# A written instruction list moved by a few places, and tiles handed out in turn, in a fused S5 and linear-attention kernel

## The chip, the core and the metric

The kernel runs on one core of one Trainium2 chip. The metric is device microseconds (us) of one execution. A core has TensorE (PE, matmuls, with its weight loads shown as PEld), VectorE (DVE), ScalarE (ACT), GpSimd (POOL) and SyncE (SP, which here only issues DMAs); POOL and ACT issue DMAs as well. Each engine works through its own instructions in their order and waits on semaphores for the others.

## The reference

One input x (2048 x 512, bf16) goes through two branches, and a gate per row mixes them:

```python
def _A_ref(x, Lambda_re, ..., Dskip):            # S5: a complex diagonal recurrence over 2048 steps
    dt = jnp.exp(log_dt)
    Lam_bar = jnp.exp(dt * Lam)
    B_bar = ((Lam_bar - 1.0) / Lam)[:, None] * Bmat
    Bu = jnp.einsum("bld,pd->blp", x + 0j, B_bar)
    for t in range(L):
        h = Lam_bar[None, :] * h + Bu[:, t, :]
    y = 2.0 * jnp.einsum("blp,dp->bld", hseq, Cmat).real + x * Dskip[None, None, :]

def _B_ref(x, wqkv, w_phi, wo):                  # linear attention, 32 heads of 16
    q, k, v = ...                                # x @ wqkv
    phi_q = concat([softmax(q @ w_phi), softmax(-q @ w_phi)])
    phi_k = concat([softmax(k @ w_phi), softmax(-k @ w_phi)])
    kv = einsum("bhsf,bhsd->bhfd", phi_k, v);  z = phi_k.sum over s
    o = (phi_q kv) / (phi_q z + 1e-6)
    return o @ wo

g = sigmoid((x * gate_w).sum(-1))
out = g * _A_ref(...) + (1 - g) * _B_ref(...)
```

## The kernel before

Everything stays on the chip between the loads at the start and the writes of the output at the end. Sequence rows are handled in 16 tiles of 128. Branch B's k, v and q come from matmuls of such tiles (`tile_mm`, L493); the feature maps work on groups of up to four tiles (`x`, `n`, `e`, `s` steps: trees of maxima and minima L544, differences L555 and L561, one exponential of 128x2048 on ACT L567, sums L575 to L586, logarithm and reciprocal L590 and L594). Branch A's input matmuls are the `b` and `g` steps (L637, L649 and on); its recurrence runs over every eighth row with scans (`z`), and the rows between are filled in by products with powers of the transition (`h`, `H`, `p`). At the end, per tile, `y` makes branch A's output in PSUM (L871, and the Dskip term with the diagonal matrix Dd, L878), `o` the attention's numerator and denominator (L890 to L903), `O` transposes that result by a DMA on SP's queue (oT<-on, L926), `t` multiplies it by Wo on top of y's bank (L939) and scales it into the output tile (L943 to L947), and `R` writes a pair of tiles out (L955, 256 KB, on SP's queue). The feature maps of q are transposed by a DMA on the same queue too (phT<-EE, L613), in the `S` steps.

What sets the order: each step is a Python generator (`st_y`, `st_t` and so on), and `ORDER` (lines 24 to 52) is a written list of 849 words. For each word the program runs the step of that name on to its next `yield`:

```python
for tok in ORDER.split():
    tok, _, banks = tok.partition("@")
    tok, _, eng = tok.partition(":")
    sel["eng"] = "dve" if eng == "D" else "act"
    sel["banks"] = [int(b) for b in banks]
    next(st[tok])
```

So `c3:D` runs the next part of `c3` with its copy on DVE, `c3` with it on ACT, and `y8@0` opens `y8` on PSUM bank 0. All engines' schedules are manual: each engine executes its instructions in the order in which the list issues them, its DMAs included. Two helpers choose the engine: `evac` (a PSUM copy, L136 on ACT, L138 on DVE) and `scaled` (a product by a per-partition scalar, L444 on ACT, L446 on DVE). `add_by_dma` (L529) adds into a tile by a DMA on POOL's queue.

At the start, small steps prepare branch A's parameters: `V` and `V2` transpose small vectors on TensorE and copy them (L330/L332, L337/L339), `P` and others compute with them on ACT and DVE, `M2` makes the products of powers on POOL (L421 to L429, nine operations, of which L425 writes scalars that the `c` steps read), and `Dk` makes Dd from Drow on POOL (L343); Drow is the row Dskip, loaded by DMA.

Tiles of five pools ("feat", "tabtmp", "ssm", "featQ", "outp") are asked from their pool each time, which rotates over a fixed number of buffers per name and waits until the buffer's last user is done.

Of the kernel before, what the change touches and what calls it, by code (L numbers as in the profile page):

```python
# [24 lines left out]
B:D Lk Lk Z@0 Lx Z Z Z Z Z Z W00@1 Z B B B W01@2 W01 W01:D W00 W00 W10@0 Lx W11@3 Lx T0@4 B W11 T0 f1@2 Lx Lx f0@1 f0  # L25
W10:D f1:D T1@5 T1:D f2@3 f2 V2@1 V2 f3@0 f3:D k0@6 x0z:D Lx k1@7 V@3 V P U U k1 k1 k0 k0 P k3@3 P2 P P2 U P2 U k6@2 P2
P2 x0 Lx Lb Lx Lb P4 n0 P4 k3 x0 P4 P3 i3 P2 n0 P3 k5@7 x0 i3 x0 Lc k5 k9@3 k9 i0 Ld Dk k2@0 M n0 i3 i3 k10@1 i3 k4@3 i0
M k2 i0 i0 i0 M Lb k10 i2 M k6 n0 k4 k7@0 k7 i2 Lb k8@7 i1 i2 x0 i1 i1 k13@6 M2 k11@0 n0 i2 k8 i1 x1 n1 x1 D n1 x1
b200@1 i2 i1 L i0:D x1 D c1:D n1 Lc Lc i3:D n1 k11 e0 b010@7 b010 c0:D x1 n1 i2:D b200 x2 s0 c0:D s0 k12@3 k12 x2 g200@2
g200 n2 c1 b100@0 s0 b100 x2 b001@5 n2 Lv b000@7 Lc i1 b000 b111@4 b111 x2 n2 s0 n2 g000@2 b001 s0 c3:D b011@3 b101@7 e1  # L30
x2 n2 g000 g000 Lx g001@5 g001 x3 s1 v1@4 b011 c3 s0 c2:D c2:D c1:D k14@2 g010@3 g010 Lo e2 x3 n3 s1 k13 D v0@0 v1 s1
g011@1 x3 c3:D g011 x3 g001 g011 v0 e2 k15@0 g011 g010 c0:D Lq Lq g010 s1 n3 k14 w2@6 c3 s0 D k15 n3 a0@54 s2 a0 g011 x3
n3 g011 Ld g010 g201@2 b101 Ld n3 s1 w2 g010 z0 b201@1 b201 z0 b110@7 n4 s1 x4 g101@3 g201 l2:D s2 s2 x4 n4 e3 z0 z0
w1@6 w1 b110 g100@2 g100 g101 g101 g100 s2 s2 s2 g111@1 l2:D l2:D g111 n4 g110@0 g110 e3 g110 g111 v2@2 v3@3 x4 n4 g110
g111 g111 g110 l2:D z0 v2 z0 v3 w3@2 s1 z0 g111 s3 g110 w0@7 w3 a1 a1 x4 c1 g301@6 z0 z1 z1 x4 w0 c2 g301 s3 g300@2 g300
z0 q3@7 q3 n4 e4 v5@6 z0 s2 s2 q2@2 s3 e4 q0@7 q0 z1 z1 l2:D z1 H0:D z1 s3 z1 z1 s4 v4@3 v4 q2 q1@0 H0 z1 v7@1 q1 X0 s3
q7@7 q7 z1 s4 N0 X0 v6@3 b300@0 N0 H0 b301@7 H0:D H0 N0 X0 v6 N0 s3 a2 v5 a2 c0 a2 v7 a2 X0 b301 s3 b300 q4@1 l3:D l3:D
l3 c2 X0 N0 H1 H1:D H1:D q4 s4 q5@0 l3 q5 q6@7 g210@6 q6 X1 N1 h0:D H1:D E0 b211@0 X1 s4 E0 b210@7 X1 s3 b210 b311@1
b310@3 g211@2 s4 N1 S0 b211 N1 S0 s4 s4 l3:D X1 g311@7 N1 s4 g210 g210 b310 g211 g211 H1 g310@3 h0 h0 h0 g210 h1:D g211
g210 h1 b311 g211 g210 h0 g211 z2 z2 S0 z2 z2 z2 z2 g311 h1 g311 g311 h1 g310 g310 g310 S0 p00 v9@2 z2 g310 g310 g311  # L40
g311 v8@6 v15@1 S0 z2 z3 v10@7 p00 v12@3 v9 v8 S0 S0 v15 v11@6 z3 z2 z2 H2 v10 q11@2 p00:D z3 z3 z3 H2 a3 a3 H2 v12 z3
H2 H2 v11 h2 p10:D z3 z3 S0 z3 a3 a3 z3 p01 X1 h1 H3 q8@3 H3 H3 q10@6 q10 v14@7 h2 h2 H3 H3 v13@1 v13 p00:D S0 h2 q11 a4
v14 N1 q9@6 h2 q9 h3:D h3:D q12@1 a4 q8 h3 q12 X2 p10 E1 E1 a4 a4 Y S0 h3 h3 Y X2 G q13@3 q13 G Y Y y1@1 y0@0 y0 N2 END
p01 y0 o0@6 p00 p11 o0 S1 o1@4 o1 q15@2 o0 p10 p10 X2 y3@3 S0 y1 p11 S1 o0 X2 N2 q15 o1 S1 o2@6 o2 N2 o2 S1 S1 y3 N2 o1
# [33 lines left out]
def kernel(  # L78
# [128 lines left out]
    ft = ft_g.__enter__()  # L207
# [69 lines left out]
    tabp = tab_g.__enter__()  # L277
    iot = tabp.tile([P, NC], F32, name="iot", bufs=1)
# [258 lines left out]
    def tree(src5, L, op, nm, key, groups=NB):  # L537
        t = ft.tile([P, 4, groups, Dh // 2, 4], BF16, name=nm)[:, 0:L]
        cur = src5
        n = Dh // 2  # L540
        while n:
            last = n == 1 and op == ALU.add
            dst = ft.tile([P, 4, groups, 1, 4], F32, name="smf", bufs=2)[:, 0:L] if last else t[:, :, :, 0:n, :]
            VT(out=dst, in0=cur[:, :, :, 0:n, :], in1=cur[:, :, :, n:2 * n, :], op=op)  # L544
# [25 lines left out]
    def feat_sum(p, L, ph=None):  # L570
        EE = live["EE", p]
        E5 = EE.rearrange("p l hh s (f hl) -> p l (hh s) f hl", f=Dh)
        sq = ft.tile([P, 2, 4 * 2 * NB, 16], BF16, name="sq")[:, :, 0:L * 2 * NB]
# [11 lines left out]
        dst = ft.tile([P, 4, 2 * NB, 1, 4], F32, name="smf", bufs=2)[:, 0:L]  # L585
# [3 lines left out]
        lg = ft.tile([P, 4, 2 * NB, 1, 4], F32, name="lg", bufs=2)[:, 0:L]  # L589
        aexp(out=lg, in_=live["sm", p], func=ACT.Ln)  # L590
        yield
        if ph is None:
            rc = ft.tile([P, 4, 2 * NB, 1, 4], BF16, name="rc", bufs=2)[:, 0:L]
            aexp(out=rc, in_=lg, func=ACT.Exp, scale=-1.0)  # L594
# [104 lines left out]
    def st_z(j):  # L699
# [17 lines left out]
        w = sw.tile([P, 2, NC], BF16, name="w")  # L717
# [17 lines left out]
    def st_h4(j):  # L735
# [3 lines left out]
        mc = sw.tile([P, 2, NC], BF16, name="mc")  # L739
# [5 lines left out]
        ms = sw.tile([P, 2, NC], BF16, name="ms")  # L745
# [22 lines left out]
    def st_h(j):  # L768
# [15 lines left out]
        m5 = sw.tile([P, 2, 2, NC], BF16, name="m5")  # L784
        n5 = sw.tile([P, 2, 2, NC], BF16, name="n5", bufs=1)
# [96 lines left out]
    def st_o(n):  # L882
# [18 lines left out]
        if u == 0:  # L901
            live["on", g_] = op_.tile([P, 2, 2, 16, Dh], BF16, name="on")
# [27 lines left out]
    def st_t(n):  # L930
# [4 lines left out]
        if u == 0:  # L935
            live["ot", g_] = pools["op"][1].tile([P, 2, D], BF16, name="ot")
        for py, (c, w) in zip(pys, [(0, D)] if len(pys) == 1 else LASTCUT):
            for g in range(HG):
                MM(out=py[:], lhsT=oT[:, g, :], rhs=Wo[:, g, c:c + w], start=False, stop=(g == HG - 1))  # L939
# [79 lines left out]
```

## Time and profile before

| | |
|---|---|
| median of 3 runs | 151.36 us (151.04 to 152.04) |
| profiled execution | 151.59 us, its span 149.9 us |
| granted TensorE clock | 1.0 |
| PE busy | 140.1 us, 94% of the span |
| DVE busy | 135.3 us, 90% |
| ACT busy | 123.5 us, 82% |
| POOL busy | 45.7 us, 30% |
| chain of waits, by engine | PE 34%, DVE 30%, ACT 12%, SP's queue 10%, DMA 7% |

The profile shows one execution. Its span goes from the first to the last instruction; 1.69 us of the execution's time lie around it. Busy shares are means over stages with different limits, so they are read by windows of time. The chain of waits is followed back from the last instruction, at each step to what released it. A wait row such as "A <- B: total, times, longest" names the instruction that waited and what came last for it.

### The profile page before, as it was taken

How to read it: one execution, taken by the hardware profiler on the slowest of the kernel's cores; microseconds unless marked ns; L12 is line 12 of the kernel's file. 1: busy time of each engine (PE TensorE's matmuls, PEld its weight loads, DVE VectorE, ACT ScalarE, POOL GpSimd, SP SyncE). 2: the span in 40 equal slices, each digit the busy share in tenths (PEclk: the TensorE clock that was granted, in tenths of full speed). 3: DMA queues.
4: the chain of work that ended last, by engine and by line, in shares of the span. 5: the costliest groups of instructions: out<-in, count | busy, mean ns of one | idle time of the engine just before them, and what ended most of it. 6: DMA issues, size and time to landing. Idle time of an engine off the chain costs nothing.

```text
span 149.9 us, 2750 instructions
## 1 busy us (share of the span) xinstructions
PE 140.1 (94%) x950; PEld 71.8 (48%) x950; DVE 135.3 (90%) x330; ACT 123.5 (82%) x222; POOL 45.7 (30%) x60
## 2 busy tenths in 40 slices
PE   6799999999799999999999998999999599999990
PEld 2644444433444644554444654545455254545650
DVE  2789979999999999999999999999999997868841
ACT  3469999899999999999999999999999958922110
POOL 7300074000229095978448163051011003000000
PEclk9999999999999999999999999999999999999999
DMA  4999999970674868679977969959998999989543
GB/s 117 221 197 195 170 201 226 215 188 0 163 120 49 127 91 119 69 112 164 154 105 132 149 83 192 155 94 164 210 219 133 104 262 158 201 162 258 112 127 118
DMA packets 56014, 22.61 MB, mean 151 GB/s; under 512 B 44736, under 2 KB 54848, under 8 KB 56000
## 3 DMA queue, kind: packets, MB, share of 16 engines
q1 hardware_dynamic: 47584, 15.05, 51.9%
q0 software_dynamic: 7472, 7.08, 33.0%
q10 hardware_dynamic: 944, 0.31, 0.8%
q8 instruction: 7, 0.11, 0.3%
q14 instruction: 7, 0.06, 0.1%
HBM read 2.51 MB, written 2.10 MB: 31 GB/s over the span
## 4 chain that ended last, share of the span: by engine, by line
PE 34%; DVE 30%; ACT 12%; SPq 10%; DMA 7%; issue 3%; POOL 2%; DVEq 0%
PE PS L871 16%; PE PS L939 9%; SPq L235 6%; DMA oT<-on 4%; DVE mn L544 4%; DVE EE L555 3%; DVE mx L544 3%; DVE EE L597 3%; DVE EE L561 3%; DVE sq L575 3%; PE PS L890 3%; DMA Drow<-in_A_Dskip_dram 3%; ACT EE L567 2%; ACT vx L136 2%; SPq L241 2%
## 5 line engine op out<-in xcount | busy, mean ns | idle before, releaser
L567 ACT ACTIVATE EE<-EE 128x2048 bf16<-128x2048 bf16 x16 | 30.1, 1918 | 0.5 <-DVE EE L561 0.4
L493 PE MATMUL PS<-WKV,xT 128*128 128x488 bf16 (+1 forms) x128 | 29.4, 374 | 0.3 <-ACT H L136 0.2
L493 PEld LDWEIGHTS <-xT 128*128 128x128 bf16 x192 | 18.4, 98 | 20.9 <-issue 1.8
L136 ACT CAST Xq<-PS 128x488 bf16<-128x488 f32 (+1 forms) x32 | 17.5, 592 | 0.2
L939 PE MATMUL PS<-Wo,oT 128*128 128x512 bf16 (+2 forms) x68 | 15.5, 367 | 1.6 <-DMA oT<-on 1.6
L649 PE MATMUL PS<-xT,BT 128*128 128x512 bf16 x64 | 16.3, 379 | 0.2 <-ACT Bn L136 0.2
L871 PE MATMUL PS<-C,H 128*128 128x512 bf16 x64 | 15.6, 379 | 0.0
L493 PE MATMUL PS<-Wq,xT 128*128 128x480 bf16 x64 | 14.9, 365 | 0.6 <-ACT vx L136 0.5
L637 PE MATMUL PS<-xT,BT 128*128 128x512 bf16 x64 | 14.8, 379 | 0.0
L903 DVE TENSOR_TENSOR on<-PS,rd 128x512 bf16<-128x512 f32 x16 | 10.9, 690 | 2.0 <-ACT rd L897 1.9
L529 POOL DMA_DIRECT2D eb<-dg x4 | 4.8, 1201 | 22.7 <-ACT dg L444 11.2
L945 ACT ACTIVATE ot<-PS,G 128x512 bf16<-128x512 f32 (+1 forms) x10 | 6.3, 648 | 6.2 <-PE PS L939 6.2
L529 POOL DMA_DIRECT2D C<-CT x4 | 6.9, 1728 | 12.8 <-DVE CT L446 12.8
L939 PEld LDWEIGHTS <-oT 128*128 128x128 bf16 x68 | 6.3, 98 | 8.5 <-DMA oT<-on 2.2
L561 DVE TENSOR_TENSOR EE<-mn,Xq 128x2048 bf16<-128x2048 bf16 (+1 forms) x9 | 9.9, 1105 | 0.0
L575 DVE TENSOR_TENSOR sq<-EE 128x2048 bf16<-128x2048 bf16 (+1 forms) x9 | 10.0, 1107 | 0.0
L555 DVE TENSOR_TENSOR EE<-Xq,mx 128x2048 bf16<-128x2048 bf16 (+1 forms) x9 | 9.9, 1105 | 0.0
L637 PEld LDWEIGHTS <-BT 128*128 128x128 bf16 x64 | 6.3, 98 | 7.7 <-issue 0.3
L597 DVE TENSOR_TENSOR EE<-EE,rc 128x2048 bf16<-128x2048 bf16 x8 | 9.7, 1221 | 0.0
L649 PEld LDWEIGHTS <-BT 128*128 128x128 bf16 x64 | 6.1, 98 | 7.2 <-issue 0.5
L894 ACT ACTIVATE ld<-PS 128x32 f32<-128x32 f32 x16 | 3.0, 201 | 8.0 <-PE PS L890 6.3
L136 ACT CAST vx<-PS 128x512 bf16<-128x512 f32 x16 | 9.3, 606 | 0.0
(193 smaller groups left out, 322.5 us busy)
## 6 DMA issues: line engine op xcount, KB each, us to landing
out_dram<-ot SPq DMA_DIRECT2D x7, 256.0 KB, 2.6
C<-CT POOLq DMA_DIRECT2D x4, 256.0 KB, 5.2
eb<-CT POOLq DMA_DIRECT2D x4, 256.0 KB, 4.5
eb<-dg POOLq DMA_DIRECT2D x4, 256.0 KB, 4.1
sq<-sq POOLq DMA_DIRECT2D x3, 256.0 KB, 4.0
WKV<-in_B_wqkv_dram SPq DMA_DIRECT2D x1, 512.0 KB, 4.8
Wo<-in_B_wo_dram SPq DMA_DIRECT2D x1, 512.0 KB, 3.9
WKV<-in_A_x_dram SPq DMA_DIRECT2D x2, 256.0 KB, 4.1
```

The costliest lines, as they stand in the source:

```text
L136: nc.scalar.copy(out=out_ap, in_=in_ap)
L493: MM(out=pt[:], lhsT=xT[:, kt, ti * P:(ti + 1) * P], rhs=W[:, kt, :], start=(kt == 0), stop=(kt == KT - 1))
L529: nc.gpsimd.dma_start(out=out_ap, in_=in_ap, accum_op=ALU.add)
L555: VT(out=half(EE, 0), in0=X5, in1=live["mx", p].to_broadcast([P, L, 8, Dh, 4]), op=ALU.subtract)
L561: VT(out=half(live["EE", p], 1), in0=live["mn", p].to_broadcast([P, L, 8, Dh, 4]), in1=X5, op=ALU.subtract)
L567: aexp(out=EE[:, l_:l_ + 2], in_=EE[:, l_:l_ + 2], func=ACT.Exp)
L575: VT(out=sq.rearrange("p q x i -> p x q i"), in0=e4[:, :, 0:2], in1=e4[:, :, 2:4], op=ALU.add)
L597: VT(out=E5[:, u:u + 2], in0=E5[:, u:u + 2], in1=rc[:, u:u + 2].to_broadcast([P, 2, 2 * NB, Dh, 4]), op=ALU.mult)
L637: MM(out=pb[:], lhsT=BT[:, ri, kt, j * P:(j + 1) * P], rhs=cells(kt, 2 * pr), start=(kt == 0), stop=(kt == KT - 1))
L649: MM(out=pgq[:], lhsT=BT[:, ri, kt, js], rhs=cells(kt, r1), start=(kt == 0), stop=(dst == 0 and j in LJ and kt == KT - 1))
L871: MM(out=py[:], lhsT=hs[j][ri], rhs=C2[:, 1 - ri, j, c:c + w], start=(j == 0 and ri == 0), stop=False)
L939: MM(out=py[:], lhsT=oT[:, g, :], rhs=Wo[:, g, c:c + w], start=False, stop=(g == HG - 1))
```

## The change

Two things change.

First, the five pools' tiles. A new helper, `rotating`, takes each name's buffers from the pool once and hands them out in turn; the number of buffers per name is the same. The later transposed feature maps get a name of their own (`phq`), and the output tile `ot` is asked for after the matmuls of `st_t`.

Second, `ORDER`. It holds the same 849 words. 264 stand at the same place, 304 one place away, 262 two, 15 three to five; four move by more (the copy of `k9` by 18 places back, `Dk` by 38 back and so behind `M2`, the copy of `k2` by 6 and `R2` by 6 forward), and the first `c3` changes its copy engine from DVE to ACT. Three steps get another PSUM bank (`V2`, `k4`, `v0`).

```diff
-W10:D f1:D T1@5 T1:D f2@3 f2 V2@1 V2 f3@0 f3:D k0@6 x0z:D Lx k1@7 V@3 V P U U k1 k1 k0 k0 P ...
+W10:D T1@5 f2@3 f1:D V2@6 V2 T1:D f2 f3@0 f3:D x0z:D k0@6 V@3 V Lx k1@7 U U P k1 k1 k0 k3@3 k0 ...
...
-o6 R0 o7@2 p20 y4 y4 o7 N3 p01 o6 o6 p20 o7 o7 y5@5 p30 E3 y5 O2 E3 y5 p20 S2 y8@0 t5 t4 p30:D y11@1 S2 R1 o9@2 p20 p20
+S2 o6 o7@2 R0 y4 o7 p20 p01 y4 N3 o6 o6 p20 o7 o7 E3 p30 y5@5 y5 y5 E3 O2 y8@0 p20 S2 y11@1 t4 t5 p30:D R1 S2 p20 p20
...
+    def rotating(pool, bufs0):
+        slots = {}
+
+        def tile_of(shape, dtype, name, bufs=None):
+            s = slots.setdefault(name, [[], 0])
+            if not s[0]:
+                s[0] = [pool.tile(shape, dtype, name=f"{name}{k}", bufs=1) for k in range(bufs or bufs0)]
+            s[1] += 1
+            return s[0][(s[1] - 1) % len(s[0])]
+
+        return tile_of
...
-    ft = ft_g.__enter__()
+    ft_tile = rotating(ft_g.__enter__(), 1)
...
-    def enter(key, **kw):
-        g = tc.tile_pool(reuse_waits="tile", **kw)
-        pools[key] = (g, g.__enter__())
+    def enter(key, name, bufs):
+        g = tc.tile_pool(name=name, bufs=1, reuse_waits="tile")
+        pools[key] = (g, rotating(g.__enter__(), bufs))
...
-        t = ft.tile([P, 4, groups, Dh // 2, 4], BF16, name=nm)[:, 0:L]
+        t = ft_tile([P, 4, groups, Dh // 2, 4], BF16, name=nm)[:, 0:L]
...
-            live["ph", g] = pools["fq"][1].tile([P, 4, NB, P], BF16, name="phT")
+            live["ph", g] = pools["fq"][1]([P, 4, NB, P], BF16, name="phq")
...
-        if u == 0:
-            live["ot", g_] = pools["op"][1].tile([P, 2, D], BF16, name="ot")
         for py, (c, w) in zip(pys, [(0, D)] if len(pys) == 1 else LASTCUT):
             for g in range(HG):
                 MM(out=py[:], lhsT=oT[:, g, :], rhs=Wo[:, g, c:c + w], start=False, stop=(g == HG - 1))
             yield
+            if u == 0 and c == 0:
+                live["ot", g_] = pools["op"][1]([P, 2, D], BF16, name="ot")
```

In the first pair of lines V's matmul (`V@3`) goes ahead of k1's first half (`k1@7`); k0 and k1 put two matmuls each into their first part. In the second pair `y11@1` goes ahead of `t4` and `t5`: four matmuls of 128x512 each.

What each engine then finds in its queue is shown at three places; line numbers of the kernel after are 12 higher from L152 on. On POOL, near the start, before (dgs and ssm_par are tiles of small parameters):

```order
L499 MEMSET Xq 128x32x4
L343 AFFINE_SELECT Dd<-Drow 128x512
L421 TENSOR_TENSOR ssm_par<-dgs,vec 128x16
L422 TENSOR_TENSOR dgs<-ssm_par 128x4
L423 TENSOR_TENSOR dgs<-ssm_par 128x4
L424 TENSOR_TENSOR dgs<-dgs,vec 128x8
L425 TENSOR_TENSOR dgs<-dgs,ssm_par 128x8
L426 TENSOR_SCALAR dgs<-dgs 128x4
L427 TENSOR_TENSOR ssm_par<-ssm_par 128x4
L428 TENSOR_TENSOR ssm_par<-ssm_par 128x4
L429 TENSOR_TENSOR ssm_par<-ssm_par 128x4
L529 DMA C_68<-CT 128x2x512
```

And after, at the same place:

```order
L511 MEMSET Xq 128x32x4
L433 TENSOR_TENSOR ssm_par<-dgs,vec 128x16
L434 TENSOR_TENSOR dgs<-ssm_par 128x4
L435 TENSOR_TENSOR dgs<-ssm_par 128x4
L436 TENSOR_TENSOR dgs<-dgs,vec 128x8
L437 TENSOR_TENSOR dgs<-dgs,ssm_par 128x8
L438 TENSOR_SCALAR dgs<-dgs 128x4
L439 TENSOR_TENSOR ssm_par<-ssm_par 128x4
L440 TENSOR_TENSOR ssm_par<-ssm_par 128x4
L441 TENSOR_TENSOR ssm_par<-ssm_par 128x4
L355 AFFINE_SELECT Dd<-Drow 128x512
L541 DMA C_68<-CT 128x2x512
```

Dd, which reads the loaded row Drow, moves from ahead of the nine M2 operations to behind them.

On ACT, from the logarithm of the second feature group on, before (EE are the feature maps, C a scaled copy of CT, H and eb results of branch A's input matmuls):

```order
L590 ACTIVATE lg<-smf 128x128
L567 ACTIVATE EE<-EE 128x2048
L136 CAST H_118<-PS 128x512
L136 CAST eb_95<-PS 128x512
L444 ACTIVATE C_68<-CT,dgs 128x512
L594 ACTIVATE rc<-lg 128x128
L567 ACTIVATE EE<-EE 128x2048
```

After:

```order
L602 ACTIVATE lg_480<-smf_469 128x128
L579 ACTIVATE EE_363<-EE_363 128x2048
L456 ACTIVATE C_68<-CT,dgs 128x512
L136 CAST H_118<-PS 128x512
L606 ACTIVATE rc_511<-lg_480 128x128
L136 CAST eb_95<-PS 128x512
L456 ACTIVATE C_68<-CT,dgs 128x512
L579 ACTIVATE EE_364<-EE_364 128x2048
```

There is one scaled copy into C more between the two exponentials, the one that DVE did before, and eb's copy stands behind rc.

On SP, near the end, where output writes and transposes share the queue, before (from the first output write, R0, on; out_0_dram is the output, on and oT the attention's result and its transpose, phT and phq the transposed feature maps):

```order
L955 DMA out_0_dram<-ot_1449 128x2x512
L926 DMA_TRANSPOSE oT_1589<-on_1515 128x8x128
L613 DMA_TRANSPOSE phT_1616<-EE_1413 128x16x128
L955 DMA out_0_dram<-ot_1498 128x2x512
L926 DMA_TRANSPOSE oT_1667<-on_1573 128x8x128
L613 DMA_TRANSPOSE phT_1616<-EE_1413 128x16x128
```

After:

```order
L967 DMA out_0_dram<-ot0_1397 128x2x512
L938 DMA_TRANSPOSE oT2_1328<-on2_1281 128x8x128
L967 DMA out_0_dram<-ot1_1398 128x2x512
L625 DMA_TRANSPOSE phq1_1407<-EE1_363 128x16x128
L938 DMA_TRANSPOSE oT3_1329<-on0_1279 128x8x128
L625 DMA_TRANSPOSE phq1_1407<-EE1_363 128x16x128
```

The second output write, R1, moves from behind the first of the transposes of S2 to ahead of it.

More of the change, by code (lines that the diff above doesn't have):

```diff
@@ L24 @@
 ORDER = """
[L25 to L44, printed above, removed]
@@ new lines @@
+i0 i0 i0 M Lb k9 i2 k10 k6 M k4 k7@0 k7 n0 Lb k8@7 i1 i2 i2 i1 i1 x0 M2 k11@0 n0 k13@6 k8 i2 Dk n1 x1 i1 x1 D x1 i2 n1
+i1 b200@1 x1 L i0:D D n1 c1:D Lc Lc n1 k11 i3:D e0 b010@7 b010 c0:D x1 n1 i2:D b200 s0 x2 s0 x2 c0:D g200@2 k12@3 k12
+g200 n2 b100@0 b100 c1 s0 n2 x2 b001@5 Lv Lc b000@7 b000 i1 b111@4 b111 s0 n2 x2 n2 g000@2 b001 s0 b101@7 e1 c3 b011@3
+x2 n2 Lx g000 g000 g001@5 g001 x3 s1 v1@4 s0 b011 c3 c2:D c2:D g010@3 g010 c1:D k14@2 Lo e2 n3 x3 D s1 v1 k13 g011@1
+v0@4 x3 s1 x3 c3:D g001 g011 g011 e2 v0 g011 k15@0 c0:D g010 Lq Lq s1 g010 n3 w2@6 k14 c3 s0 D k15 a0@54 n3 a0 g011 s2
@@ L276 @@
     tab_g = tc.tile_pool(name="tabtmp", bufs=2, reuse_waits="tile")
-    tabp = tab_g.__enter__()
-    iot = tabp.tile([P, NC], F32, name="iot", bufs=1)
+    tab_tile = rotating(tab_g.__enter__(), 2)
+    iot = tab_tile([P, NC], F32, name="iot", bufs=1)
     identf = stg.tile([P, P], F32, name="identf", bufs=1)
@@ L542, in tree @@
             last = n == 1 and op == ALU.add
-            dst = ft.tile([P, 4, groups, 1, 4], F32, name="smf", bufs=2)[:, 0:L] if last else t[:, :, :, 0:n, :]
+            dst = ft_tile([P, 4, groups, 1, 4], F32, name="smf", bufs=2)[:, 0:L] if last else t[:, :, :, 0:n, :]
             VT(out=dst, in0=cur[:, :, :, 0:n, :], in1=cur[:, :, :, n:2 * n, :], op=op)
@@ L552, in feat_max @@
         yield from tree(X5, L, ALU.max, "mx", ("mx", p))
-        EE = ft.tile([P, 4, NB, 2, 64], BF16, name="EE", bufs=3)[:, 0:L]
+        EE = ft_tile([P, 4, NB, 2, 64], BF16, name="EE", bufs=3)[:, 0:L]
         live["EE", p] = EE
@@ L584, in feat_sum @@
         yield
-        dst = ft.tile([P, 4, 2 * NB, 1, 4], F32, name="smf", bufs=2)[:, 0:L]
+        dst = ft_tile([P, 4, 2 * NB, 1, 4], F32, name="smf", bufs=2)[:, 0:L]
         VT(out=dst.rearrange("p l g o hl -> p (l g) (o hl)"), in0=t[:, :, 0:4], in1=t[:, :, 4:8], op=ALU.add)
@@ L588, in feat_sum @@
         yield
-        lg = ft.tile([P, 4, 2 * NB, 1, 4], F32, name="lg", bufs=2)[:, 0:L]
+        lg = ft_tile([P, 4, 2 * NB, 1, 4], F32, name="lg", bufs=2)[:, 0:L]
         aexp(out=lg, in_=live["sm", p], func=ACT.Ln)
@@ L592, in feat_sum @@
         if ph is None:
-            rc = ft.tile([P, 4, 2 * NB, 1, 4], BF16, name="rc", bufs=2)[:, 0:L]
+            rc = ft_tile([P, 4, 2 * NB, 1, 4], BF16, name="rc", bufs=2)[:, 0:L]
             aexp(out=rc, in_=lg, func=ACT.Exp, scale=-1.0)
@@ L703, in st_z @@
         V = vv[j][:, :, NC:N2]
-        mc = sw.tile([P, 2, NC], BF16, name="mc")
+        mc = sw([P, 2, NC], BF16, name="mc")
         VT(out=mc[:], in0=V, in1=c2, op=ALU.mult)
         yield
-        ms = sw.tile([P, 2, NC], BF16, name="ms")
+        ms = sw([P, 2, NC], BF16, name="ms")
         VT(out=ms[:], in0=V, in1=s2, op=ALU.mult)
@@ L716, in st_z @@
         rb = r8_[:, j:j + 1].to_broadcast([P, NC])
-        w = sw.tile([P, 2, NC], BF16, name="w")
+        w = sw([P, 2, NC], BF16, name="w")
         for ri in range(2):
@@ L721, in st_z @@
         hz = H3[:, j, :, ZP:ZP + NC]
-        mc = hz if j in ZD else sw.tile([P, 2, NC], BF16, name="mc")
+        mc = hz if j in ZD else sw([P, 2, NC], BF16, name="mc")
         VT(out=mc, in0=w[:], in1=c2, op=ALU.mult)
         yield
-        ms = sw.tile([P, 2, NC], BF16, name="ms")
+        ms = sw([P, 2, NC], BF16, name="ms")
         VT(out=ms[:], in0=w[:], in1=s2, op=ALU.mult)
@@ L738, in st_h4 @@
         hn = H3[:, j, :, ZP + NC:ZP + N2]
-        mc = sw.tile([P, 2, NC], BF16, name="mc")
+        mc = sw([P, 2, NC], BF16, name="mc")
         scaled(mc[:], prev, dgs[:, S_NR, j:j + 1])
@@ L744, in st_h4 @@
             yield
-        ms = sw.tile([P, 2, NC], BF16, name="ms")
+        ms = sw([P, 2, NC], BF16, name="ms")
         if j in HD:
@@ L783, in st_h @@
             return
-        m5 = sw.tile([P, 2, 2, NC], BF16, name="m5")
-        n5 = sw.tile([P, 2, 2, NC], BF16, name="n5", bufs=1)
+        m5 = sw([P, 2, 2, NC], BF16, name="m5")
+        n5 = sw([P, 2, 2, NC], BF16, name="n5", bufs=1)
         scaled(m5[:], prevs(j), dgs[:, S_MR, j:j + 1])
@@ L901, in st_o @@
         if u == 0:
-            live["on", g_] = op_.tile([P, 2, 2, 16, Dh], BF16, name="on")
+            live["on", g_] = op_([P, 2, 2, 16, Dh], BF16, name="on")
         VT(out=live["on", g_][:, u], in0=pn[:, :, :, 0:Dh], in1=rd[:].unsqueeze(3).to_broadcast([P, 2, 16, Dh]), op=ALU.mult)
@@ L913, in st_O @@
         L = len(OGROUPS[g])
-        oT = pools["op"][1].tile([P, 2, HG, P], BF16, name="oT", bufs=4)
+        oT = pools["op"][1]([P, 2, HG, P], BF16, name="oT", bufs=4)
         for u in range(L):
```

43 lines of the change are left out of this document (29 added, 14 removed).

## The prediction

> **What bounds the kernel now.** First I read the windows, cut where the work changes: the middle, the stretch in which TensorE is full, a hole, and the end. Columns are busy time of PE, its weight loads, DVE, ACT and POOL, then TensorE's granted clock, the DMA share and GB/s.
>
> ```profile
> core 0: us, PE busy (x) PEld busy (x) DVE busy (x) ACT busy (x) POOL busy (x), PEclk, DMA share, GB/s
> 28.50:92.90 64.40, 62.33 (x416) 31.31 (x414) 64.37 (x138) 62.66 (x109) 32.20 (x31) 1.00 0.74 121
> 92.90:117.90 25.00, 24.99 (x192) 13.24 (x191) 24.93 (x54) 24.42 (x43) 3.60 (x3) 1.00 1.07 157
> 117.90:119.70 1.80, 0.21 (x2) 0.05 (x2) 1.80 (x5) 1.80 (x2) 0.00 (x0) 1.00 0.55 106
> 119.70:145.90 26.20, 26.20 (x200) 14.10 (x200) 20.49 (x37) 11.91 (x28) 1.20 (x1) 1.00 0.86 182
> ```
>
> In the middle three engines are nearly full at once: DVE idles 0.03 us, ACT 1.74, PE 2.07. After 92.9 PE has no gap but the hole at 117.9. The clock is whole throughout. So the time comes down only where all three gain in the middle, or where PE's hole closes. Which waits stand there, the chain of waits says (start, length, what):
>
> ```profile
> 15.71 3.86 DMA Drow<-in_A_Dskip_dram
> 19.64 1.13 POOL Dd L343
> 20.77 1.00 POOL ssm_par L421
> ...
> 22.78 0.35 DVE C L446
> ...
> 92.86 0.97 PE PS L493 x4
> ...
> 113.34 6.27 DMA oT<-on
> 119.66 1.90 PE PS L939 x8
> 121.56 0.86 PE PS L871 x4
> ```
>
> Two places are a transfer that an engine sits out: Drow's, which holds POOL and through it DVE, and oT's, which holds PE. Between them the chain runs on DVE and ACT up to 92.86 and on PE from there. The waits, over the whole span for DVE and PE (first two rows) and of ACT in 28.5 to 92.9 (the rest); the columns are total, times, longest:
>
> ```profile
> DVE C L446 <- POOL dgs L425: 1.1, 1, 1.1
> PE PS L939 <- DMA oT<-on: 1.6, 1, 1.6
> ACT lg L590 <- DVE smf L586: 0.6, 1, 0.6
> ACT vv L136 <- PE PS L671: 0.4, 1, 0.4
> ACT phT L444 <- DMA H<-ms: 0.3, 1, 0.3
> ACT EE L567 <- DVE EE L561: 0.2, 1, 0.2
> ACT Bn L136 <- PE PS L637: 0.2, 1, 0.2
> ```
>
> These make up 1.7 of ACT's 1.74 idle us.
>
> **The change part by part.** The tiles handed out in turn keep their number, size and users, and no engine gets an instruction from it: 0. The bound is a wait for a tile's last reader: none of the waits above is one, so nothing can be gained, and I take 0 for a loss as the turn is the same. The work is the same but for one scaled copy that goes from DVE to ACT. All else is order.
>
> *Head.* V's small transposing matmul (L330) stood behind four k matmuls on TensorE and now stands behind two. V's copy and P follow it:
>
> ```profile
> 8.43 0.98 PE L493 MATMUL PS<-WKV,xT 128*128 128x488 bf16 x4
> 9.35 0.18 PE L330 MATMUL PS<-ident,vec_n 12*128 12x12 bf16 x1
> 9.56 0.17 DVE L332 CAST vec<-PS 128x12 f32<-128x12 bf16 x1 [0.38 <-PE PS L330]
> 9.77 0.20 ACT L358 ACTIVATE ssm_par<-vec 128x4 f32<-128x4 f32 x1 [1.35 <-DVE vec L332]
> ```
>
> L330 comes (9.35 − 8.43)/2 = 0.46 us earlier, DVE waited 0.38 for it and ACT 1.35, so both take it: −0.46 on ACT, about that on DVE. Bounds: 0, if the loads or copies it also needs come last, and 0.92, if V could go right at 8.43.
>
> *Dk behind M2 on POOL.* M2's first operation (20.77) no longer waits for Dd, which waits for Drow until 19.57. The wait of DVE for L425 (1.1 us) goes, if M2's inputs are there by then. Among the operations on that tile, this row has the last write of them (min, median and max in ns, first and last start):
>
> ```profile
> L415 DVE TENSOR_SCALAR dgs<-dgs x1: 166/166/166, 15.9 to 15.9; 128x12 f32<-128x12 f32 x1
> ```
>
> So M2 can run from about 16.1 on; what is late next is DVE itself. Dd moves back by the part of M2 that DVE waits for (20.77 to 22.78, 2.0 us); its readers are the L878 matmuls, far later than this. DVE: −1.10, bounds 0 and −1.10.
>
> *c3 on ACT.* One copy C<-CT,dgs leaves DVE (0.35 by the row at 22.78) and goes to ACT. From the start of the same form on ACT to the next instruction:
>
> ```profile
> 32.12 0.73 ACT L444 ACTIVATE C<-CT,dgs 128x512 bf16<-128x512 bf16 x1
> 32.75 0.30 ACT L594 ACTIVATE rc<-lg 128x128 bf16<-128x128 f32 x1
> ```
>
> That is 0.63 us more on ACT, 0.35 less on DVE. ACT's wait for smf at lg (0.6 by its row) lies just before: DVE is ahead by 1.10 + 0.46 there, so that wait goes, −0.6. Bounds 0 to −0.6.
>
> *ACT's other waits.* H1's add goes ahead of c2's on POOL's queue, so the 0.3 us for H goes; the 0.2 for DVE's EE goes as DVE leads. For the 0.4 and 0.2 that hang on PE I take nothing: on PE g010 and k14, k11 and k13, v0 and g011 change places, each waiting for another bank's copy, and PE's 2.07 us of gaps bound both a gain and a loss. −0.5, bounds 0 and −1.1.
>
> *The middle in sum.* DVE gains 1.10 + 0.46 + 0.35 = 1.91, ACT 0.46 + 0.6 − 0.63 + 0.5 = 0.93, PE can follow as far as 2.07. The least decides: −0.93. Bounds: −1.53 (0.46 + 0.6 − 0.63 + 1.1) and +0.63 (c3 alone).
>
> *Tail.* On PE y11's first four matmuls (0.86 by the chain's row at 121.56) go ahead of t4 and t5, into the hole in which t5 waits for oT. If oT lands as before, PE loses 0.86 less: −0.86. Bounds −1.76 (117.90 to 119.66, oT in time) and the cost of what moves on SP's queue: the output write R1 now stands ahead of a transpose into phT instead of behind it, and R2 and O8 move up likewise. PE reads that transpose at the L890 row:
>
> ```profile
> 115.28 3.89 SPq L613 DMA_TRANSPOSE phT<-EE  x1
> 119.26 0.53 SPq L955 DMA_DIRECT2D out_dram<-ot  x1
> ...
> 122.26 0.42 PE L890 MATMUL PS<-KVm,phT 128*128 128x68 bf16 x8
> ```
>
> ```profile
> phT<-EE SPq DMA_TRANSPOSE x1, 5.9
> out_dram<-ot SPq DMA_DIRECT2D x1, 256.0 KB, 2.6
> ```
>
> The transpose lands at 115.28 + 5.9 = 121.2, 1.06 before use; with y11 gone from between, 0.2 is left. R1's issue (0.53) fits in SP's idle time ahead of 115.28, but 2.6 us of its packets run beside the transposes. A push of up to 0.2 is free; I take that, and count a larger one as a rival.
>
> *Sum.* 151.59 (profiled execution: span 149.9 and 1.69 around it) − 0.93 − 0.86 = 149.80. The median of the runs shown, 151.36, is 0.23 below that execution: 149.6.
>
> One row bears on why oT takes 6.3 us; the first below is from the DMA view of 116 to 118, and the second, from 118 to 120, oT's next transfer:
>
> ```profile
> q8 instruction: 1, 0.02, 5.3%
> oT<-on SPq DMA_TRANSPOSE x1, 3.3
> ```
>
> One packet of instructions took 5.3% of 16 engines over 2 us, that is 1.7 us of one engine, in the very time in which oT was late by 6.3 − 3.3 = 3.0 us. The Trainium skill ("Runtime: NRT & Kernel Launch", Instruction fetch mechanics) says that crossing a fetched 16 KiB block of instructions is mostly hidden. By that rule the packet is not the cause, the sum would stay at 149.6 or lose more to the write moved beside the transposes; the trace here leaves it open.
>
> **The rivals.**
>
> *All of it closes* (ACT's waits all go, oT lands in time): 151.59 − 1.53 − 1.76 = 148.30, 148.1 on the median's scale. For it: the head moves oT's producers as well. Against: oT's lateness lies in the transfer, not in its start. 0.12.
>
> *ACT carries nothing.* c3's 0.63 meets a head gain that the next wait swallows (0.63 against 0.46), and the lg wait only moves to PE's banks. Only 0.86 is left: 150.73, so 150.5. For it: ACT and PE together have under 2.1 us of gaps in 64, and the places on PE that were swapped wait for ACT's copies. 0.22.
>
> *POOL's operations now hold DVE.* M2 ran while DVE stood still for 1.10 us; now it runs beside DVE's work. What this looks like here:
>
> ```profile
> 20.18 0.63 DVE L544 TENSOR_TENSOR mx<-mx 128x64 bf16<-128x64 bf16 x1
> 23.32 0.19 DVE L544 TENSOR_TENSOR mn<-mn 128x64 bf16<-128x64 bf16 x1
> ```
>
> The same form took 0.63 during Dd and 0.19 later. At the most DVE gives back M2's 2.0 us, and its 1.91 is gone: the middle gains nothing or loses 0.1, the tail keeps 0.86: 150.7 to 150.8, so 150.5 as a median. The Trainium skill ("SBUF — State Buffer", Who interferes with whom) has this as a lock: a DVE operation with two SBUF inputs and a GpSimd one that reads SBUF exclude each other for a whole instruction, and the first comer wins. By that rule each M2 operation can hold DVE once. 0.08, since eight of M2's nine operations are small.
>
> *The write pushes the transposes* (slower). R1's 2.6 us go wholly ahead of the transpose: it lands at 123.8, PE's L890 at 122.26 waits 1.54 beyond its old time, and the middle's 0.93 doesn't cover that: 151.59 + 1.54 − 0.93 = 152.2; where ACT carries nothing either, 153.1. On the median's scale 152.0 to 152.9. It is slower than before from a push of 1.06 + 0.93 = 1.99 us on. For it: the transposes there take 5.9 and 6.3 against 3.3. Against: R1 then goes out when SP is idle, and it leaves the time after 119.26, where O3 stands behind it. 0.13.
>
> **How the numbers follow.** The forecast has 0.45, with its own range 148.9 to 150.4 (the head's and ACT's bounds by half). The rivals have 0.12, 0.22, 0.08 and 0.13. The range 148.0 to 151.4 holds the forecast, all that closes (most of it), ACT carrying nothing and DVE held, and leaves out the write and a few strays of each: about 0.8. A measurement of this kernel can tell about 1% from no change, that is 149.85 and 152.87. Faster by more: 0.32 of the forecast, 0.12, and 0.05 of the others: 0.49. Slower by more: 0.09, most of it the write with strays of the swapped PE places. Same: 0.42.
>
> **What would show it.** Head: ACT's P starts near 9.3. Dk: DVE has no wait for POOL's dgs, and Dd stands behind M2. c3: an ACT row C<-CT,dgs right after the second exponential, and no wait of lg for smf. Middle: the first k/q matmuls of the full stretch (92.86) come near 91.9; if they don't, ACT's wait rows name what swallowed it. Tail: the wait of L939 for oT is about 0.7, and L890 after it doesn't wait for phT. The prediction is wrong if PE's gaps in the middle grow beyond 2.07, if DVE's operations beside M2 are much over their later length, or if phT lands over 1 us later than y11 allows.

## The result and the profile after

The changed kernel takes 150.37 us (median of 22 runs, 150.1 to 152.54), the kernel before 152.06 us in runs beside it (median of 22, 151.04 to 152.68). The ratio is 0.991, 95% interval 0.9891 to 0.9929: 1.4 us less by the ratio, where 1.76 were forecast. The median before is 0.7 us above the 151.36 that the prediction started from; executions of that program lie mostly near 151.15 and 152.05, and the profiled one (151.59) is between. The profiled execution after took 150.44 us, its span 148.7.

The windows of the kernel after, at the same cuts as before and with the same columns:

```profile
28.50:92.90 64.40, 62.75 (x416) 32.19 (x420) 64.14 (x134) 63.55 (x110) 32.42 (x31) 1.00 0.77 124
92.90:117.90 25.00, 24.62 (x189) 13.23 (x191) 24.93 (x53) 24.06 (x43) 3.60 (x3) 1.00 0.97 162
117.90:119.70 1.80, 1.80 (x10) 0.84 (x9) 1.80 (x6) 1.80 (x3) 0.00 (x0) 1.00 1.30 181
119.70:145.90 26.20, 24.20 (x187) 12.80 (x187) 20.39 (x36) 11.63 (x29) 1.20 (x1) 1.00 0.85 174
```

TensorE's hole at 117.9 is full now (1.80 of 1.80). The last window holds a new one: TensorE is busy for 24.20 of 26.20 us, and of the rest about 0.9 is only the earlier end of the work. The waits: DVE has none for POOL's dgs any more. Of the rows below, the first three are all that the view lists of ACT's in the middle (28 to 92), the next two are TensorE's longest behind the start of the kernel, and the last is POOL's before Dd.

```profile
ACT lg L602 <- DVE smf L598: 0.4, 1, 0.4
ACT vx L136 <- PE PS L505: 0.2, 1, 0.2
ACT CT L456 <- DMA eb<-CT: 0.2, 1, 0.2
PE PS L902 <- DMA phq<-EE: 1.0, 1, 1.0
PE PS L638 <- ACT vx L136: 0.9, 2, 0.6
POOL Dd L355 <- DMA Drow<-in_A_Dskip_dram: 2.5, 1, 2.5
```

The wait for oT (1.6) is gone, and one of 1.0 for the transposed feature maps phq has come. POOL still sits before Dd, but with M2 done.

Where the time went is best read from one engine that is full: the start of the same step's matmuls on TensorE (of their first weight load) in a run's profile, less that in the profile before. A minus means earlier; the text calls it TensorE's lead. The columns name the step and its time in us. The same table serves the experiments.

| profile of | k8, near 17 | g010, near 40 | q13, near 92 | y8, near 117 | t6, near 124 | t15, near 145 | ratio to before, 95% interval |
|---|---|---|---|---|---|---|---|
| after | −0.17 | −1.06 | −0.89 | −0.69 | −2.37 | −0.85 | 0.991 (0.9891–0.9929) |
| tiles_only | −0.01 | −0.01 | +0.42 | +0.42 | +0.48 | +0.48 | 1.0014 (0.9995–1.0034) |
| head_only | −0.18 | −0.19 | +0.25 | +0.26 | +0.23 | +0.23 | 1.0004 (0.9978–1.0029) |
| tail_only | 0.00 | 0.00 | +0.23 | +0.14 | −1.33 | +0.01 | 0.9988 (0.9969–1.0006) |
| dk_behind | +0.04 | −1.11 | −1.11 | −1.10 | −1.05 | −1.05 | 0.9913 (0.9888–0.9938) |
| after_dk_ahead | −0.18 | −0.98 | −0.92 | −0.73 | −2.44 | −0.85 | 0.9923 (0.9896–0.9949) |
| dk_c3act | −0.02 | −0.92 | −0.71 | −0.71 | −1.44 | −1.44 | 0.9875 (0.9836–0.9913) |
| front_only | −0.18 | −1.08 | −1.01 | −0.84 | −1.55 | −1.55 | 0.9859 (0.9836–0.9882) |
| front_c3dve | −0.19 | −1.33 | −1.37 | −1.21 | −1.97 | −1.82 | 0.9861 (0.9825–0.9898) |
| front_y11 | −0.18 | −1.08 | −1.25 | −1.08 | −2.08 | −2.06 | 0.9839 (0.9815–0.9863) |
| two_moves | +0.17 | −0.98 | −0.53 | −0.52 | −1.02 | −1.02 | 0.9896 (0.9861–0.9932) |
| r2_behind | −0.18 | −1.08 | −1.17 | −0.99 | −2.76 | −1.22 | 0.9896 (0.987–0.9922) |
| late_before | −0.19 | −1.11 | −1.31 | −1.11 | −2.83 | −1.82 | 0.9889 (0.9859–0.9919) |

The row of tiles_only has the order of before, so its +0.42 at q13 is what two executions of one order can differ by: a ratio from many executions decides whether something was gained, and a profile tells where. After the change TensorE leads by 0.89 at its full stretch, gains 1.68 more at the hole (−0.69 to −2.37) and gives 1.52 of it back by the end.

### The profile page after: what moved, and what is told of

The parts are those of the page before. It is cut to its first block, busy times and chain, and to the rows that moved or that the text cites. A ratio compares the mean times of both kernels' runs of the same rounds, so it can differ in the third digit from the quotient of the medians.

```text
span 148.7 us, 2730 instructions
## 1 busy us (share of the span) xinstructions
PE 139.5 (94%) x937; PEld 71.7 (48%) x950; DVE 135.7 (91%) x329; ACT 123.5 (83%) x223; POOL 44.8 (30%) x60
## 4 chain that ended last, share of the span: by engine, by line
DVE 56%; DMA 12%; issue 12%; POOL 8%; ACT 5%; PE 5%; SPq 1%; POOLq 0%; DVEq 0%; ACTq 0%
DVE mx L556 7%; DVE mn L556 6%; DVE on L915 5%; DVE sq L587 5%; DMA eb<-CT 4%; DVE EE L567 4%; DMA phq<-EE 4%; DVE EE L573 4%; POOL H L541 4%; DMA mc<-ms 2%; DVE dg L449 2%; DVE EE L621 2%; DVE sq L592 2%; ACT CT L456 1%; DMA out_dram<-ot 1%
## 5 line engine op out<-in xcount | busy, mean ns | idle before, releaser
L883 PE MATMUL PS<-C,H 128*128 128x512 bf16 x60 | 15.1, 379 | 0.2
L541 POOL DMA_DIRECT2D C<-CT x4 | 7.4, 1844 | 15.6 <-DVE CT L458 15.6
```

Of the source, the lines that this page charges most:

```text
L541: nc.gpsimd.dma_start(out=out_ap, in_=in_ap, accum_op=ALU.add)
```

## The experiments

All of them have the tiles handed out in turn and differ in the written list only.

**The tiles alone** (tiles_only): the list of before.

```diff
 ORDER = (the list of before)
+    def rotating(pool, bufs0):  ... as in the change
```

> The list of before, with the tiles handed out in turn and the output tile asked for later: nothing of the order changes. My theory: no engine's queue differs, so 1.000 of before, within 0.3%. Rival: the way the tiles are handed out takes away waits of its own and carries the gain: 0.991, as the whole change.

1.0014 (0.9995 to 1.0034): nothing. All that the change does is order.

**Front and tail apart** (front_only, tail_only): the cut is after word 588, just ahead of the first y steps.

```diff
-ORDER = after
+ORDER = after[:588] + before[588:]      # front_only
+ORDER = before[:588] + after[588:]      # tail_only
```

> The first 588 words of the list as after, the rest (from the first y steps on) as before. My theory: TensorE's lead of 0.7 to 0.9 us at the start of the full stretch is made here and carried to the end, hole included: 0.994 to 0.996 of before. Rival 1: the hole at oT swallows the lead (the transfer lands when it landed): 1.000. Rival 2: the front carries all of the gain: 0.991.

> The first 588 words as before, the rest as after. My theory: the hole at oT closes (1.6 us less on TensorE), but the wait of o14's matmuls for the transposed feature maps (1.0 us) comes in its place near the end: a net of 0.0 to 0.6 us, 0.996 to 1.000 of before, and the trace shows the one wait gone and the other there. Rival: the tail carries its hole whole, 0.989.

The front alone gives 0.9859, more than the whole change, and the two intervals lie apart: every expectation was too small, the rival's 0.991 too. The tail alone gives 0.9988, no change that can be told, by the two waits that were expected: at the first place TensorE runs through, and at the second it waits. Timeline of tail_only, TensorE, at the hole and near o14:

```profile
117.18 1.89 PE L883 MATMUL PS<-C,eb 128*128 128x512 bf16 x8
118.90 1.89 PE L949 MATMUL PS<-Wo,oT 128*128 128x512 bf16 x8
...
138.47 0.43 PE L902 MATMUL PS<-KVm,phq 128*128 128x68 bf16 x8 [1.05 <-DMA phq<-EE]
```

In front_only the wait for oT is there, but shorter (0.89 us for 1.59), and that is where TensorE's lead grows from 0.84 to 1.55. Nothing waits at o14, and the lead stays at 1.55 to the end:

```profile
118.11 1.25 PE L949 MATMUL PS<-Wo,oT 128*128 128x512 bf16 x5 [0.89 <-DMA oT<-on]
```

**One word: Dk behind M2** (dk_behind), and undone in the whole change (after_dk_ahead).

```diff
-... i0 Ld Dk k2@0 M n0 ... k13@6 M2 k11@0 n0 ...      # before
+... i0 Ld k2@0 M n0 ... k13@6 M2 Dk k11@0 n0 ...      # dk_behind
-... x0 M2 k11@0 n0 k13@6 k8 i2 Dk n1 ...              # after
+... x0 Dk M2 k11@0 n0 k13@6 k8 i2 n1 ...              # after_dk_ahead
```

> The list of before with one word moved: Dk right behind M2. My theory: DVE's 1.10 us for POOL's dgs goes, with it ACT's 0.57 us for smf and TensorE's 0.68 us for a0's input, and 0.4 to 0.7 us reach the end: 0.995 to 0.997 of before. Rival 1: ACT or TensorE holds, nothing reaches the end: 1.000. Rival 2: this one swap is the front's whole gain: 0.986.

> The kernel after with one word moved back: Dk ahead of M2 on POOL. My theory: the swap is the one part of the change that pays; without it DVE waits its 1.1 us for POOL again, and the rest, front and tail together, gives nothing: 0.999 to 1.003 of before. Rival: the change gains in several places, each enough alone (the full DVE and ACT are relieved by the other shifts too): 0.994 or less.

Moving the one word gives 0.9913, as much as the whole change and a larger gain than the 0.995 to 0.997 that I expected. The table shows it whole: TensorE is 1.11 us earlier at g010 and stays so to the end. The size is that of DVE's wait, 1.10 us, which is gone in this run. Of ACT's five waits in the middle two are left in that run:

```profile
ACT phT L456 <- DMA H<-ms: 0.2, 1, 0.2
ACT EE L579 <- DVE EE L573: 0.2, 1, 0.2
```

Yet my theory fell in the other direction: with Dk back ahead of M2 the change keeps its gain (0.9923, where 0.999 to 1.003 was expected). DVE's wait is there again, but half as long, 0.52 us by its row, since POOL's operations took other times. POOL's and DVE's rows of that run:

```profile
19.63 0.63 POOL L355 TENSOR_SCALAR_AFFINE_SELECT Dd<-Drow 128x512 bf16<-128x512 bf16 x1 [11.10 <-DMA Drow<-in_A_Dskip_dram]
20.24 0.24 POOL L433 TENSOR_TENSOR ssm_par<-dgs,vec 128x16 f32<-128x16 f32 x1
...
20.71 0.91 POOL L435 TENSOR_TENSOR dgs<-ssm_par 128x4 f32<-128x4 f32 x1
```

```profile
19.67 0.74 DVE L556 TENSOR_TENSOR mn<-mn 128x256 bf16<-128x256 bf16 x1
...
20.58 0.98 DVE L449 TENSOR_TENSOR dg<-ident,dgv 128x1536 bf16<-128x1536 bf16 x1
...
22.22 0.35 DVE L458 TENSOR_SCALAR C<-CT,dgs 128x512 bf16<-128x512 bf16 x1 [0.52 <-POOL dgs L437]
```

Dd and M2's first operation took 0.87 us together, against 1.13 and 1.00 before. DVE's first large difference behind the wait starts at 22.98 instead of 23.69, 0.71 us earlier, and 0.58 of that is the shorter wait. At q13 TensorE is where it is in the whole change (−0.92 and −0.89). So the swap is enough by itself, and beside the other shifts it is not needed. That half of DVE's wait was gone without the swap is part of it; which of the other shifts makes up the rest was not tested one by one.

**c3 on ACT** (dk_c3act: with Dk alone; front_c3dve: taken back in the front).

```diff
-s0 c3:D b011@3 b101@7 e1          # dk_behind
+s0 b011@3 b101@7 e1 c3            # dk_c3act
-e1 c3 b011@3                      # front_only
+e1 c3:D b011@3                    # front_c3dve
```

> Dk behind M2, and the first c3's copy on ACT behind the second exponential instead of on DVE, the rest as before. My theory: ACT is the nearer bound there, 0.63 us later than with Dk alone, less what DVE's 0.35 gives: TensorE 0.2 to 0.6 us later at the full stretch, 0.993 to 0.995 of before against 0.991 with Dk alone. Rival: DVE is the bound; 0.989.

> The front as after but for the first c3, whose copy stays on DVE as before; the rest as before. My theory: ACT saves 0.63 us behind the second exponential and DVE pays 0.3; ACT is the nearer bound there, so 0.1 to 0.5 us less than the front alone: 0.982 to 0.985 of before. Rival: DVE is the bound once M2 no longer holds it; the copy costs its 0.3 us there: 0.988.

The first read 0.9875 where 0.993 to 0.995 was expected, and its interval overlaps that of Dk alone; the second 0.9861 against 0.9859 with the flip. In the profiles the flip costs TensorE 0.19 and 0.25 us at g010 (−0.92 against −1.11, −1.08 against −1.33), but the ratios tell no loss. In dk_c3act TensorE's wait for oT is 0.86 us instead of 1.65 in dk_behind, so its lead doubles there (−0.71 at y8, −1.44 at t6). Why oT comes sooner is shown under the rivals below; it is not the price of the copy, with which the theory dealt.

**The head alone** (head_only): the first 90 words.

```diff
-ORDER = before
+ORDER = after[:90] + before[90:]
```

> The first 90 words of the list as after (V's matmul behind two k matmuls, its copy ahead; V2 on another bank), the rest as before, Dk ahead of M2 too. My theory: ACT's P starts 0.5 us earlier, but the copy of k1 behind it waits for its matmuls, so ACT keeps 0.16 us: 0.999 to 1.000 of before. Rival: the head's 0.46 us goes through the middle to the end: 0.997.

1.0004: nothing. The kernel after shows why, and head_only has the same two rows within 0.02 us. ACT's rows after:

```profile
9.19 0.20 ACT L370 ACTIVATE ssm_par<-vec 128x4 f32<-128x4 f32 x1 [0.76 <-DVE vec L344]
9.91 1.04 ACT L136 CAST Xq<-PS 128x488 bf16<-128x488 f32 x2 [0.52 <-PE PS L505]
```

P starts at 9.19 instead of 9.77, and then ACT waits 0.52 us for the k matmuls whose results it copies next (at 9.91; before, at 10.08). Of 0.58 it keeps 0.17.

**y11 in the hole** (front_y11: on the front; two_moves: with Dk alone).

```diff
-y8@0 t5 t4 p30:D y11@1 S2
+y8@0 y11@1 t5 t4 p30:D S2
```

> The front as after, the rest as before, and of the tail only y11's first four matmuls ahead of t5 and t4. My theory: the 0.89 us that TensorE waits for oT in the run with the front alone are filled by 0.86 us of matmuls, and SP's queue stays as before, so no wait for phq comes in its place: 0.6 to 0.9 us less than the front alone, 0.980 to 0.982 of before. Rival: TensorE, earlier by 0.86 us, waits for the next transposes into phq or oT, or for banks that DVE frees: 0.985 to 0.986 as the front alone.

> The list of before with two moves only: Dk right behind M2, and y11's first four matmuls ahead of t5 and t4. My theory: 1.1 us from the first, carried to the end; of TensorE's 1.65 us for oT 0.86 are filled, and the transposes keep their places on SP's queue, though the one into phq, 0.2 us ahead of its use then, may take 0.3 to 0.5 back: 1.5 to 2.0 us, 0.987 to 0.990 of before, and not slower than the whole change. Rival: y11's matmuls only move the wait (as SP's queue sets the tail): 0.992, as with Dk alone.

The ratios are 0.9839 and 0.9896, each a little under the run without the move (0.9859, 0.9913), but the intervals overlap, so neither pair decides between theory and rival. The profile of front_y11 shows what is left of 0.89: the wait for oT is gone, and 0.55 us are waited for the transpose into phq that the prediction had 0.2 us ahead of its use. In two_moves the wait for oT falls from 1.65 to 0.82 us, yet its profile ends with a lead of 1.02 us, no more than dk_behind's 1.05: it had only 0.53 at q13.

```profile
117.72 1.90 PE L949 MATMUL PS<-Wo,oT 128*128 128x512 bf16 x8
120.17 0.43 PE L902 MATMUL PS<-KVm,phq 128*128 128x68 bf16 x8 [0.55 <-DMA phq<-EE]
```

front_y11 has the lowest time of all, 149.39 us, 0.7% under the whole change by the two ratios, whose intervals lie apart.

**What gives the hole back** (r2_behind, late_before).

```diff
-t8 R2 S3 y12@0 o12 ...            # after
+t8 S3 R2 y12@0 o12 ...            # r2_behind
-ORDER = after
+ORDER = after[:791] + before[791:]      # late_before
```

> The kernel after, with one swap: the output write R2 behind the last transpose into phq instead of ahead of it. My theory: R2's 256 KB slowed that transpose (6.1 us against 4.6 before); behind it the transpose starts 0.6 us earlier and lands 1 to 2 us earlier, and TensorE's wait of 1.02 us at o14 goes. What is late next is DVE and ACT at the end, so 0.6 to 1.0 us less than after: 0.984 to 0.987 of before. Rival: the transposes are slow there for another reason (a packet of instructions, the transposes beside them); the wait stays: 0.991, as after.

> The kernel after, but its last 58 words (from t8 on, with R2 and the steps o14, o15, t10 and y13) in the order of before. My theory: the last 58 words are where the tail gives its hole back (the wait of 1.0 us at o14, R2 ahead of the last transpose into phq, and o15's matmuls ahead of the copy that frees their bank); with them as before TensorE keeps the 2.0 to 2.4 us that it leads by at t6, and the result is 0.982 to 0.986 of before. Rival: the loss is made earlier in the tail, by R1 ahead of the transposes of S2 and the changed order round O3; then it stays at 0.990.

The wait at o14 goes in both, and the one swap of r2_behind shows its cause: with R2 ahead of it on SP's queue the last transpose into phq lands 6.1 us after its issue, with R2 behind it 4.6. The DMA view's row of the kernel after, then of r2_behind:

```profile
phq<-EE SPq DMA_TRANSPOSE x1, 6.1
```

```profile
phq<-EE SPq DMA_TRANSPOSE x1, 4.6
```

It is so in every profile: 6.1 in the three with R2 ahead (after, tail_only, after_dk_ahead), 4.4 to 4.9 in the eleven others. But r2_behind is no faster than the kernel after: 0.9896, where 0.984 to 0.987 was expected. Its write goes out later, so t10's product on DVE waits 1.53 us for the output buffer that the write still reads. By TensorE's row, that product in turn holds the PSUM bank for which TensorE waits 0.89 us:

```profile
137.27 0.75 DVE L955 SCALAR_TENSOR_TENSOR ot<-PS,G,xd 128x512 bf16<-128x512 f32 x1 [1.53 <-DMA out_dram<-ot]
```

```profile
138.07 0.29 PE L902 MATMUL PS<-KVm,phq 128*128 128x68 bf16 x4 [0.89 <-DVE ot L955]
```

late_before puts o15's matmuls back behind y12's too. In its profile TensorE loses 1.01 us from t6 to the end (2.83 to 1.82), where the kernel after loses 1.52. So the last 58 words account for about 0.5 us of the loss there, and not for all of it as I had thought; two waits for a bank that DVE's `on` holds are another 0.5 in that run. The ratio, 0.9889, misses my 0.982 to 0.986, and its interval overlaps the whole change's, so the time itself does not show even the 0.5.

## Why the prediction held, and where it did not

**The forecast** was 149.6 us or 1.2% less. The ratio says 0.9%, which is 150.0 us on the scale of 151.36: inside the range, 0.4 us above the forecast and 0.5 below the two rivals at 150.5. The number alone doesn't tell them apart, the profiles do. They show that the sum came out near by luck in part: of its two terms of about 0.9, one arrived, by another way than forecast, and the other arrived almost twice over and was lost again.

**Tiles: 0.** Right (1.0014).

**Dk behind M2, −1.10 on DVE.** Right, and the only term that reached the end in full: alone it takes 1.11 us off TensorE from g010 on. The prediction cut DVE's gain to what ACT could follow ("the least decides"); for this term alone nothing was cut.

**Head, −0.46 on ACT.** Failed. The wait for V got shorter, by 0.58 us on ACT, but ACT's next wait, for the k matmuls (0.52), took all but 0.17 of it. The prediction priced the instruction that moved, not what stood behind it on ACT.

**c3, +0.63 on ACT, and the wait for smf, −0.6.** On ACT the sizes were right. ACT's timeline before, at the logarithm and at the second exponential from there, and the same two after:

```profile
29.16 0.31 ACT L590 ACTIVATE lg<-smf 128x128 f32<-128x128 f32 x1 [0.57 <-DVE smf L586]
...
32.95 1.90 ACT L567 ACTIVATE EE<-EE 128x2048 bf16<-128x2048 bf16 x1
```

```profile
28.26 0.39 ACT L602 ACTIVATE lg<-smf 128x128 f32<-128x128 f32 x1
...
32.65 1.98 ACT L579 ACTIVATE EE<-EE 128x2048 bf16<-128x2048 bf16 x1
```

Without the wait ACT is 0.90 us earlier, and behind c3 it is 0.30 earlier, so c3 took 0.60. At the end it costs nothing that the ratios can tell.

**The middle in sum, −0.93.** TensorE is 0.89 us earlier at q13. The number was right, the way was not: Dk alone gives 1.11 there, and the other shifts of the front give nothing beyond it that can be told from the 0.42 by which two executions differ. They take waits away and add others (smf for another lg 0.4, eb for CT 0.2, vx for TensorE 0.9). That the front is faster by 0.5% than Dk alone all the same lies, in the profiles, at oT: TensorE's lead there grows from 0.84 to 1.55.

**Tail, −0.86.** This is the step that failed. The hole gave 1.68 us, near its bound of 1.76: y11's matmuls filled 0.86 of it as forecast, and the rest came because oT landed 5.0 us after its issue instead of 6.3, which the prediction took as unchanged. Of the 1.68, 1.52 was lost again by the end, so the tail gave 0.16 by the profile, and by itself (tail_only) nothing that can be told. The DMA views at that place after:

```profile
oT<-on SPq DMA_TRANSPOSE x1, 5.0
...
phq<-EE SPq DMA_TRANSPOSE x1, 6.0
```

The prediction counted R1 ahead of the second of these, where no push came (5.9 us before, 6.0 after), and passed over R2 with "move up likewise". There the rival's mechanism, a write that pushes a transpose, cost 1.5 us of landing and 1.0 of TensorE's time. Moving R2 alone did not bring that back (r2_behind), and where the rest of the 1.52 is lost is known only in part.

**The rivals.** POOL holding DVE: in the kernel after M2 runs from 13.96 to 16.73 beside DVE's work, and DVE's lead goes from 0.16 (the same operation at 13.64 for 13.80) to 0.11 (15.83 for 15.94): not so. ACT carrying nothing: not so, since the middle did gain. All closing: the hole did, not the rest.

The packet of instructions was left open by the prediction, and the traces speak for it. Two such packets fall into oT's transfer before, one on queue q8 and one on q14; the prediction's window, from 116 on, held only the one on q8. The two runs that differ only by the first c3 show the difference. This is the DMA view of dk_behind in 112.2 to 118.6, from oT's issue to its landing (GB/s in 40 slices of 0.16 us):

```profile
GB/s 0 45 179 166 166 186 160 134 128 192 179 119 147 205 221 229 205 178 150 269 200 147 18 0 0 5 6 10 10 10 118 269 187 8 8 8 6 10 235 298
q14 instruction: 1, 0.01, 1.7%
q8 instruction: 1, 0.02, 0.9%
oT<-on SPq DMA_TRANSPOSE x1, 6.3
```

And dk_c3act in 112.6 to 117.9 (slices of 0.13 us), where the packet on q14 starts only at 117.99:

```profile
GB/s 0 8 162 178 178 147 193 170 162 100 162 178 193 116 120 162 220 228 224 222 203 176 143 155 342 228 185 48 0 0 0 8 10 10 8 10 10 73 292 110
q8 instruction: 1, 0.02, 1.0%
oT<-on SPq DMA_TRANSPOSE x1, 5.5
```

With two packets the transfers nearly stop twice, with one once, and oT is 0.8 us sooner. TensorE's wait for it follows, first in dk_behind, then in dk_c3act:

```profile
118.61 1.90 PE L949 MATMUL PS<-Wo,oT 128*128 128x512 bf16 x8 [1.65 <-DMA oT<-on]
```

```profile
118.22 1.90 PE L949 MATMUL PS<-Wo,oT 128*128 128x512 bf16 x8 [0.86 <-DMA oT<-on]
```

All fourteen profiles fit this. In the five in which both packets come before oT is done (before, tiles_only, head_only, dk_behind, two_moves) the transposes' packets stand still for 2.4 to 2.6 us in all and oT takes 6.2 to 6.4. In the other nine only the one on q8 does, and the packets stand still for 1.5 to 1.6 us. Of these, oT takes 5.4 to 5.6 in dk_c3act, front_only, front_c3dve and front_y11, and 4.8 to 5.1 in the five with the tail of after or most of it. The last difference lies ahead of the stop: oT's first packet moves 3.3 us after POOL's transfer into eb was issued in every profile, and in those five oT is issued 0.2 to 0.4 us later behind that issue. No run moves a packet by itself, so this is read from the traces and not tested, and why the packets fall where they do is open.

The Trainium skill ("Runtime: NRT & Kernel Launch", Instruction fetch mechanics) calls the cost of crossing a 16 KiB block of instructions mostly hidden; at this place it was not: TensorE waited 1.65 us for oT in dk_behind, with two packets in the transfer, and 0.86 in dk_c3act, with one. So part of what the new order gains, the 0.7 us that the front adds at oT above all, is luck: nothing in the list was written for it.

## What to carry to other kernels

In a list that keeps three engines full, look first for an instruction that waits for a transfer ahead of short work that others need: one word moved gave what the whole rewritten list of 849 words gave. A transfer that is moved ahead of another on a full queue has to be priced at each place where it happens, and so has what stands behind a wait that goes: the gains of the head, of y11 and of R2's swap were all taken, in part or whole, by the very next wait. Cutting a reordered list into a front and a tail, and running each half beside the old other half, shows in two runs which half pays; here the front alone (0.9859) is better than front and tail together (0.991).

## What the runs showed of the hardware

At three places here, of a POOL operation and a DVE operation with two inputs in SBUF that start within 0.15 us of each other, the second ends only just behind the first. In the profile before, M2's first operation (20.77, 1.00 us) began just behind this one of DVE, and ended just behind it:

```profile
20.74 0.95 DVE L437 TENSOR_TENSOR dg<-ident,dgv 128x1536 bf16<-128x1536 bf16 x1
```

The same operation of M2 takes 0.24 us in after_dk_ahead, where the one that meets dg (20.58, 0.98) is the 128x4 product of L435, 0.91 us instead of 0.2 as in the kernel after. The other way round, in the same run, Dd on POOL (19.63, 0.63) ends at 20.26, and DVE's 128x256 minimum, begun at 19.67, at 20.41 after 0.74 us; in the kernel after it runs behind Dd and takes 0.28:

```profile
20.19 0.28 DVE L556 TENSOR_TENSOR mn<-mn 128x256 bf16<-128x256 bf16 x1
```

This is the lock of the Trainium skill ("SBUF — State Buffer", Who interferes with whom) as the prediction quoted it: the first comer has the port for the whole instruction. Which operation is caught changes here with some tenths of a us, and so a wait of 1.10 us became one of 0.52 with the same two steps in the same order on POOL.

A DMA transpose under way nearly stops for a while when a packet of instructions is fetched. In the profiles from 100 to 131 us a transpose's packet of 256 bytes takes 18 ns in the median and 99% take under 70, but those caught behind a packet on q8 take up to 1.4 to 1.6 us, and those behind one on q14 up to 0.5 to 0.9. In these fourteen profiles each such fetch that met transposes in full flow there was followed by such a stop.
